# Attention, SiLU layer and rational layer on one core: forty instead of 23 products of zeros, and a new order of the work

## The chip, the core and the metric

One core of a Trainium2 chip. The time is device microseconds of one execution. The engines are PE (TensorE: products, and loads of its stationary operand), DVE (VectorE), ACT (ScalarE), POOL (GpSimd) and SP, which issues the DMAs. Each engine works through its own queue in order; semaphores tie the queues together.

## The reference

Input are 4 batches x 8 heads x 768 tokens with x (32 wide), a, B and C (16 wide). Three stages follow one another:

```
# attention, sub-chunks of 32 tokens, per batch and head
L = exp(cum_i - cum_j) for i >= j;  M = (C B^T) * L
y = M x + (C state) * exp(cum)
state = exp(sum la) * state + sum_j B_j x_j * exp(cum_end - cum_j)
# the heads side by side: 3072 tokens x 256
x1 = silu(y @ w_in) @ w_out                        # 256 -> 2048 -> 256
h  = x1 @ w_in2
x2 = (a0 + a1 h + a2 h^2 + a3 h^3) / (1 + |b0||h| + |b1| h^2 + 1e-6) @ w_out2
```

The kernel gets the layers' weights as 64-bit floats, and the rest as 32-bit floats.

## The kernel before

**Tiling.** The 3072 tokens are 24 chunks of 128. Attention goes chunk by chunk: C B^T and the masks (tile M, L700, two per chunk), the state (S and um, L780 to L792), y; y leaves as a high part y1h (ACT, L802) and a low part y1l (DVE, L805). Layer 1 runs over seven blocks of 2, 2, 4, 4, 4, 4, 4 chunks, and in each over sixteen slices f of 128 hidden units: 256 inputs to 128 hidden units (tile h), SiLU on ACT (L888), its high part gh (L844 on ACT or L846 on POOL) and low part gl (L850 on DVE or POOL), and the product back to 256 outputs, summed in acc over the slices. The first two blocks are 256 tokens wide, so their products are 128x256, the others 128x512. Layer 2 does the same over six blocks of 512 tokens with the rational function.

**Three products for one.** Each fp32 operand of the layers is split into a high and a low half that TensorE takes at full precision, and a product is hi·hi + lo·hi + hi·lo (in_proj L813, out_proj L819). All products are issued by mm, so they all show as L280.

**Weights.** A slice of weights arrives as 64-bit words (wraw, L472, 512 KB), becomes fp32 (wv) by one ACT instruction (L489) and two of DVE (L495, L497, below: the decode pair), and is split into the high half (ACT, L513) and the low half (L517, on POOL or DVE). A product with slice f needs both. The names w0 to w15 are the sixteen slices of layer 1. Factors Ee of later chunks are stored to memory (dre, L443) and loaded back spread out (L579); SP issues these and all other DMAs in one queue.

**The order.** No engine's order is written out by hand. Each step is handed to a planner (class Plan) with a list of engines that may do it, a cost on each, what it depends on, and a key. The planner runs a clock of its own: of all steps that could start soonest it takes the one with the smallest key, and this fixes the order of every engine before the program is built. The keys are sums of due times and of the numbers in the dictionary K (L31 to L69).

**Products of zeros.** K["warm"] steps are products of a 128x128 by a 128x512 tile of zeros in bf16, into a bank that is not in use (L452 to L460). POOL clears the zeros once (T, L450). Their key is 99.0, and each may begin from a time of its own on the planner's clock:

```
    for i in range(int(K["warm"])):
        ...
            mm(acc_t[1], z[:, 0:P], z[:, 0:512], True, True)
        add({"PE": (0.215, f_warm)}, 99.0, [o_zero], use=[zeros, spare], cols=512, after=K["warm0"] + K["warmstep"] * i)
```

In the trace they show as acc<-T, in the order as acc1<-T.

Of the kernel before, what the change touches and what calls it, by code (L numbers as in the profile page):

```python
# [28 lines left out]
HALVED = 0  # L29
TAIL_FLEX = 1  # L30
K = dict(  # L31
    t0=-18.163,
    step0=2.86,
    lag1=43.503,
    fo1=10.942,
    fo2=4472.323,
    fol=32.531,
    tab=-80.822,
    lead=168.696,
    kt=-12.237,  # L40
    kq=-77.043,
    kl=20.552,
    kg=62.898,
    ks=777.795,
    warm=23,
    warm0=5.147,
    warmstep=0.414,
    late=46.508,
    tab0=-2757.678,
    bulk=-58.119,  # L50
    d0=-14.734,
    gap0=36.588,
    d2=-19.542,
    d3=2.257,
    early2=9.278,
    early=24.026,
    w2a=-1512.003,
    w2b=-160.848,
    w1=-1.707,
    w1step=-31.741,  # L60
    w1load=3869.872,
    tokload=-233.083,
    ahead=17.68,
    eps=0.031,
    step2=168.582,
    dT=[-64.27, 36.68, -1.66, 34.6, -29.6, -174.18, 35.5, -3.13, -9.78, 138.44, -41.72, -26.53],
    dD=[-124.33, -53.44, 1.94, -60.08, -128.23, 35.27, -89.78, -84.57],
    dW=[28.05, -44.69, -91.49, 180.41, 166.11, 92.54, 19.47, 34.68, 21.96, 122.42, 25.71, 20.72, -50.06, -0.22, -24.39, 76.24],
)  # L69
SET_LN_EXP, SET_SILU = 6, 18  # L70

# [1098 lines left out]
```

## Time and profile before

| | |
|---|---|
| runs, us | 610.43, 612.09, 612.76; median 612.09 |
| profiled execution, us | 611.65, its span 609.9 |
| mean granted clock of TensorE | 0.985 |
| PE busy | 597.7 us, 98% of the span |
| DVE, ACT, POOL busy | 441.9, 401.2, 375.8 us |

The profile is of one execution. The span runs from its first to its last instruction; the time of the execution is 1.75 us more. A stretch's granted clock of 1.00 is TensorE's upper level, 2.4 GHz, 0.50 its lower, 1.2 GHz. In a row of a timeline neighbouring instructions of one kind stand together (x4), with the time from the first's start to the last's end, and in brackets the idle time before them and what ended it.

### The profile page before, as it was taken

The numbers are of one execution on the slowest core, as the hardware profiler recorded it, in microseconds if no ns is written. First come the engines' busy times: TensorE is split into PE (matmuls) and PEld (weight loads), VectorE is DVE, ScalarE is ACT, GpSimd is POOL, SyncE is SP. The second block draws the span as 40 slices with busy tenths as digits, with TensorE's granted clock in tenths as the row PEclk, the third lists the DMA queues.
The fourth block names the chain that finished last, engine by engine and source line by source line (L and its number), as shares of the span: only waits on it lengthen the run. The fifth ranks groups of instructions, "written<-read, shape, count | busy, mean of one in ns | idle before, by whom it ended". The sixth has DMA issues, their size and how long they took to land.

```text
span 609.9 us, 9980 instructions
## 1 busy us (share of the span) xinstructions
PE 597.7 (98%) x3501; PEld 478.6 (78%) x3505; DVE 441.9 (72%) x740; ACT 401.2 (66%) x782; POOL 375.8 (62%) x493
## 2 busy tenths in 40 slices
PE   7799999999999999999999999999999999999997
PEld 4478798887777777777888888888888788878875
DVE  5799988665344435432313899999999999999994
ACT  5678777554333333322335898989988988898893
POOL 5878846205344444222201599899889889889984
PEclk8599999999999999999999999999999999999999
DMA  7765778751111000000036600000000000000000
GB/s 258 227 199 209 234 250 286 243 200 37 46 28 36 23 21 27 1 2 1 1 104 199 250 0 1 36 1 1 35 1 2 34 1 1 35 1 1 35 2 34
DMA packets 18314, 47.30 MB, mean 78 GB/s; under 512 B 2136, under 2 KB 5336, under 8 KB 18264
## 3 DMA queue, kind: packets, MB, share of 16 engines
q1 hardware_dynamic: 18264, 46.67, 23.1%
q8 instruction: 27, 0.44, 0.3%
q14 instruction: 23, 0.19, 0.1%
HBM read 34.99 MB, written 11.67 MB: 77 GB/s over the span
## 4 chain that ended last, share of the span: by engine, by line
PE 88%; DVE 4%; DMA 4%; ACT 2%; issue 1%; SPq 0%; DVEq 0%; ACTq 0%
PE acc L280 42%; PE h L280 35%; PE b L280 7%; PE att L280 4%; DMA wraw<-in_w_dram 3%; DMA Ee<-dre 1%; DVE wv L497 1%; DVE w L517 1%; ACT wv L489 1%; DVE M L700 1%; DVE wv L495 0%; DVE gl L850 0%; ACT w L513 0%; DVE tok L613 0%; DVE y1l L805 0%
## 5 line engine op out<-in xcount | busy, mean ns | idle before, releaser
L280 PE MATMUL h<-y1h,w 128*128 128x512 f32 (+1 forms) x700 | 229.4, 377 | 2.3 <-DVE gl L850 1.9
L280 PE MATMUL acc<-gh,w 128*128 128x512 f32 (+1 forms) x832 | 213.1, 377 | 0.2 <-ACT gh L844 0.2
L280 PEld LDWEIGHTS acc<-gh,w 128*128 128x128 f32 x832 | 149.4, 188 | 30.6 <-POOL gh L846 0.4
L280 PEld LDWEIGHTS h<-y1h,w 128*128 128x128 f32 x700 | 129.7, 189 | 31.9 <-DVE gl L850 3.0
L850 DVE TENSOR_TENSOR gl<-T,gh 128x512 fp32r<-128x512 f32 x79 | 57.4, 727 | 116.0 <-POOL gh L846 84.8
L280 PE MATMUL h<-y1l,w 128*128 128x512 f32 (+1 forms) x350 | 130.8, 374 | 0.0
L850 POOL TENSOR_TENSOR gl<-g,gh 128x512 fp32r<-128x512 f32 x95 | 123.1, 1300 | 11.5 <-ACT gh L844 4.5
L280 PE MATMUL acc<-gl,w 128*128 128x512 f32 (+1 forms) x416 | 123.8, 378 | 0.0
L846 POOL TENSOR_SCALAR gh<-T 128x512 fp32r<-128x512 f32 x54 | 33.9, 627 | 137.2 <-ACT T L888 106.7
L888 ACT ACTIVATE T<-h 128x512 f32<-128x512 f32 x80 | 47.7, 597 | 97.6 <-PE h L280 91.8
L280 PEld LDWEIGHTS acc<-gl,w 128*128 128x128 f32 x416 | 75.9, 188 | 16.1
L953 POOL TENSOR_SCALAR tok<-T,abt 128x512 f32<-128x512 f32 x96 | 74.7, 778 | 16.3 <-ACT T L945 13.1
L280 PEld LDWEIGHTS h<-y1l,w 128*128 128x128 f32 x350 | 66.4, 190 | 11.6 <-DVE y1l L805 0.2
L956 DVE SCALAR_TENSOR_TENSOR b<-T,absb,b 128x512 f32<-128x512 f32 x96 | 71.9, 749 | 2.9 <-ACT b L949 2.6
L965 ACT ACTIVATE b<-b,lnb 128x512 f32<-128x512 f32 x96 | 64.1, 667 | 14.6 <-DVE b L956 14.6
L974 DVE SCALAR_TENSOR_TENSOR g<-tok,abt,b 128x512 f32<-128x512 f32 x96 | 71.3, 742 | 2.3 <-POOL gl L850 1.3
L590 POOL TENSOR_SCALAR_AFFINE_SELECT Gm<-eG 128x256 f32<-128x256 f32 x96 | 52.4, 581 | 9.8 <-ACT eG L386 6.0
L968 ACT ACTIVATE b<-b 128x512 f32<-128x512 f32 x96 | 56.8, 592 | 0.3
L962 DVE SCALAR_TENSOR_TENSOR tok<-T,abt,h 128x512 f32<-128x512 f32 x63 | 46.8, 743 | 0.9
L280 PE MATMUL b<-y1h,w 128*128 128x512 f32 x132 | 46.4, 392 | 0.0
L959 DVE TENSOR_TENSOR h<-tok,h 128x512 f32<-128x512 f32 x63 | 43.2, 686 | 0.0
L949 ACT ACTIVATE b<-h,abt 128x512 f32<-128x512 f32 x63 | 42.0, 667 | 0.9 <-DVE g L974 0.5
(76 smaller groups left out, 687.6 us busy)
## 6 DMA issues: line engine op xcount, KB each, us to landing
wraw<-in_w_dram SPq DMA_DIRECT2D x32, 512.0 KB, 5.1
w2s<-wraw SPq DMA_DIRECT2D x16, 512.0 KB, 3.4
w<-w2s SPq DMA_DIRECT2D x16, 512.0 KB, 4.2
tok<-in_tok_dram SPq DMA_DIRECT2D x24, 320.0 KB, 3.2
out_dram<-Gm SPq DMA_DIRECT2D x12, 256.0 KB, 2.0
Ee<-dre SPq DMA_DIRECT2D x21, 66.5 KB
cum<-in_consts_dram SPq DMA_DIRECT2D x1, 320.0 KB, 3.1
dre<-Ee SPq DMA_DIRECT2D x2, 66.5 KB
```

The costliest lines, as they stand in the source:

```text
L280: PE.matmul(out, lhsT, rhs, start=start, stop=stop)
L590: POOL.affine_select(g4[:, :, p * SUB : (p + 1) * SUB], eG[:, p, n * H : (n + 1) * H].unsqueeze(2).broadcast_to([P, H, SUB]), pattern=[[0, ...
L850: eng.tensor_tensor(gl.t[:, 0:W], g.t[:, 0:W], gh.t[:, 0:W], op=ALU.subtract)
L888: ACT.activation(T.t[:, 0:W], h.t[:, 0:W], AF.Silu)
L949: ACT.activation(c.t[:, 0:W], h.t[:, 0:W], AF.Abs, scale=abt[:, 4:5])
L953: POOL.tensor_scalar(t1.t[:, 0:W], s.t[:, 0:W], abt[:, 3:4], abt[:, 1:2], op0=ALU.mult, op1=ALU.add)
L956: DVE.scalar_tensor_tensor(c.t[:, 0:W], s.t[:, 0:W], absb[:, 1:2], c.t[:, 0:W], op0=ALU.mult, op1=ALU.add)
L959: DVE.tensor_tensor(h.t[:, 0:W], t1.t[:, 0:W], h.t[:, 0:W], op=ALU.mult)
L962: DVE.scalar_tensor_tensor(t1.t[:, 0:W], s.t[:, 0:W], abt[:, 2:3], h.t[:, 0:W], op0=ALU.mult, op1=ALU.add)
L965: ACT.activation(c.t[:, 0:W], c.t[:, 0:W], AF.Ln, bias=lnb)
L968: ACT.activation(c.t[:, 0:W], c.t[:, 0:W], AF.Exp, scale=-1.0)
L974: DVE.scalar_tensor_tensor(g.t[:, 0:W], t1.t[:, 0:W], abt[:, 0:1], c.t[:, 0:W], op0=ALU.add, op1=ALU.mult)
```

## The change

The dictionary K is replaced; no other line differs. warm goes from 23 to 40, the other numbers are keys (all but warm0 and warmstep differ):

```
-    t0=-18.163,
-    step0=2.86,
+    t0=-6.161,
+    step0=4.251,
...
-    warm=23,
+    warm=40,
     warm0=5.147,
     warmstep=0.414,
...
-    dD=[-124.33, -53.44, 1.94, -60.08, -128.23, 35.27, -89.78, -84.57],
+    dD=[-156.62, -40.06, -8.38, -62.34, -108.32, 38.34, -55.21, -111.62],
```

Every engine gets a new order. Apart from those of zeros the products on PE are the same as before, and the same ones stand ahead of slice 13 of block 0 and of slice 4 of block 1. In the names below the first number tells the tile and is the same in both programs where the tile is; the last number is a running one.

On PE, between slice 12 of block 0 (h_268) and its slice 13 (h_271), before:

```order
L280 MATMUL h_268_881<-y1h_67,w12_58_852 128x256 x2
L280 MATMUL h_268_881<-y1l_68,w12_58_852 128x256
L280 MATMUL h_268_881<-y1h_67,w12_58_852 128x256
L280 MATMUL h_271_895<-y1h_67,w13_61_865 128x256
L280 MATMUL h_271_895<-y1l_68,w13_61_865 128x256
L280 MATMUL h_271_895<-y1h_67,w13_61_865 128x256 x2
L280 MATMUL h_271_895<-y1l_68,w13_61_865 128x256
L280 MATMUL h_271_895<-y1h_67,w13_61_865 128x256
L280 LDWEIGHTS T_15_91
L280 MATMUL acc1_73<-T_15_91 128x512
```

Slice 13's products follow slice 12's at once, and five products of zeros (T_15) stand behind them, of which the first is shown. The same place after the change, from the last two of eleven products of zeros on:

```order
L280 LDWEIGHTS T_15_91
L280 MATMUL acc1_73<-T_15_91 128x512
L280 LDWEIGHTS T_15_91
L280 MATMUL acc1_73<-T_15_91 128x512
L280 MATMUL h_271_940<-y1h_67,w13_61_912 128x256
L280 MATMUL h_271_940<-y1l_68,w13_61_912 128x256
L280 MATMUL h_271_940<-y1h_67,w13_61_912 128x256 x2
L280 MATMUL h_271_940<-y1l_68,w13_61_912 128x256
L280 MATMUL h_271_940<-y1h_67,w13_61_912 128x256
L280 LDWEIGHTS T_15_91
```

Eleven products of zeros now stand between the two slices, and one follows; six more stand directly ahead of slice 12. In all 34 instead of 18 stand ahead of slice 13, and 40 instead of 23 ahead of slice 4 of block 1.

On DVE, what stands just ahead of the low half (L517) of slice 13 before:

```order
L497 SCALAR_TENSOR_TENSOR wv_57_755<-wraw_56_684,wv_57_755 128x512
L495 TENSOR_SCALAR wv_60_810<-wv_60_810 128x512
L850 TENSOR_TENSOR gl_267_854<-h_265_787,gh_266_820 128x256
L497 SCALAR_TENSOR_TENSOR wv_60_810<-wraw_59_751,wv_60_810 128x512
L517 TENSOR_TENSOR w12_58_852<-wv_57_755,w12_58_852 128x512
L517 TENSOR_TENSOR w13_61_865<-wv_60_810,w13_61_865 128x512
L805 TENSOR_TENSOR y1l_68<-att0_80,y1h_67 128x2x128
L788 TENSOR_TENSOR um_117_890<-att1_81,con_60 128x64
L700 TENSOR_TENSOR M_115_893<-att0_80,Gm_113_713 128x512
```

and after:

```order
L495 TENSOR_SCALAR wv_60_837<-wv_60_837 128x512
L805 TENSOR_TENSOR y1l_68<-att0_80,y1h_67 128x2x128
L700 TENSOR_TENSOR M_115_867<-att0_80,Gm_113_743 128x512
L700 TENSOR_TENSOR M_116_878<-att1_81,Gm_113_743 128x512
L850 TENSOR_TENSOR gl_267_884<-h_265_842,gh_266_872 128x256
L497 SCALAR_TENSOR_TENSOR wv_60_837<-wraw_59_778,wv_60_837 128x512
L495 TENSOR_SCALAR wv_63_894<-wv_63_894 128x512
L792 SCALAR_TENSOR_TENSOR S_114_915<-S_108_794,Ee_106_451,um_117_851 128x64
L497 SCALAR_TENSOR_TENSOR wv_63_894<-wraw_62_839,wv_63_894 128x512
L517 TENSOR_TENSOR w13_61_912<-wv_60_837,w13_61_912 128x512
L517 TENSOR_TENSOR w14_64_929<-wv_63_894,w14_64_929 128x512
```

The low half of slice 12 has left DVE for POOL, and two masks of chunk 8 (M_115, M_116), a state update (S_114) and slice 14's decode pair (wv_63) have moved ahead of slice 13's low half. Counted from the start, 107 instructions instead of 93 stand ahead of it.

On POOL, the early low halves of slices 1 and 2 before:

```order
L607 TENSOR_TENSOR tok_73_161<-tok_73_161,eL_66 128x128
L517 TENSOR_TENSOR w1_25_211<-wv_24_183,w1_25_211 128x512
L590 AFFINE_SELECT Gm_74_238<-eG_65 128x8x32 x4
L629 TENSOR_TENSOR tok_73_161<-tok_73_161,Ee_12_202 128x128
L517 TENSOR_TENSOR w2_28_258<-wv_27_226,w2_28_258 128x512
```

and on DVE after:

```order
L495 TENSOR_SCALAR wv_27_226<-wv_27_226 128x512
L517 TENSOR_TENSOR w1_25_217<-wv_24_183,w1_25_217 128x512
L497 SCALAR_TENSOR_TENSOR wv_27_226<-wraw_26_185,wv_27_226 128x512
L788 TENSOR_TENSOR um_78_245<-att1_81,con_60 128x64
L700 TENSOR_TENSOR M_71_250<-att0_80,Gm_69_178 128x512
L517 TENSOR_TENSOR w2_28_248<-wv_27_226,w2_28_248 128x512
```

The low halves of slices 1, 2, 3, 5, 7 and 9 move from POOL to DVE, and those of 11 and 12 the other way. In the rest of the kernel 41 high parts gh move from POOL to ACT, and the attention of chunks 12 to 15 moves to an earlier place. On SP the load of chunk 4's tokens now stands ahead of the first store of dre instead of behind it.

## Rows read from the trace of the kernel before

**Rows 1.** Page: busy time; tenths of 40 slices, ACT and clock.
```profile
PE 597.7 (98%) x3501; PEld 478.6 (78%) x3505; DVE 441.9 (72%) x740; ACT 401.2 (66%) x782; POOL 375.8 (62%) x493
...
ACT  5678777554333333322335898989988988898893
...
PEclk8599999999999999999999999999999999999999
```
**Rows 2.** Stretches: us, busy of PE, PEld, DVE, ACT, POOL; clock; DMA; GB/s.
```profile
15.00:28.50 13.50, 11.48 (x93) 6.92 (x90) 10.96 (x22) 8.44 (x19) 11.88 (x20) 0.50 0.76 229
30.00:45.00 15.00, 14.70 (x166) 11.47 (x167) 13.99 (x30) 10.81 (x27) 11.16 (x15) 1.00 0.66 203
45.00:60.00 15.00, 14.56 (x180) 12.36 (x178) 14.44 (x31) 12.54 (x36) 12.63 (x22) 1.00 0.65 216
60.00:75.00 15.00, 13.83 (x164) 11.58 (x161) 13.93 (x31) 11.80 (x32) 11.98 (x17) 1.00 0.66 218
75.00:90.00 15.00, 15.00 (x164) 14.27 (x157) 13.15 (x30) 12.73 (x35) 6.11 (x11) 1.00 0.75 244
```
**Rows 3.** Timeline of PE: start, us, instruction, idle before and what ended it.
```profile
24.98 0.58 PE L280 MATMUL h<-y1h,w 128*128 128x256 f32 x1
...
30.23 0.39 PE L280 MATMUL h<-y1h,w 128*128 128x256 f32 x1 [1.25 <-DVE gl L850]
...
34.59 1.03 PE L280 MATMUL acc<-T 128*128 128x512 bf16 x4
35.59 0.71 PE L280 MATMUL att<-tok 32*128 32x256 f32 x8
...
58.58 0.40 PE L280 MATMUL h<-y1h,w 128*128 128x256 f32 x2
...
59.65 1.03 PE L280 MATMUL acc<-T 128*128 128x512 bf16 x4
...
75.12 0.39 PE L280 MATMUL h<-y1h,w 128*128 128x256 f32 x1
```
**Rows 4.** Timeline of DVE, same columns.
```profile
29.55 0.29 DVE L613 TENSOR_TENSOR tok<-tok,Ee 128x128 f32<-128x128 f32 x1 [1.33 <-DMA Ee<-dre]
...
55.82 0.67 DVE L497 SCALAR_TENSOR_TENSOR wv<-wraw,wv 128x512 uint32<-128x512 uint32 x1
56.42 1.74 DVE L517 TENSOR_TENSOR w<-wv,w 128x512 fp32r<-128x512 f32 x2
```
**Rows 5.** DVE by lines, 15 to 75 us: count, busy us, mean ns, idle before.
```profile
L497 DVE SCALAR_TENSOR_TENSOR wv<-wraw,wv 128x512 uint32<-128x512 uint32 x17 | 12.9, 758 | 0.1
L700 DVE TENSOR_TENSOR M<-att,Gm 128x512 f32<-128x512 f32 x18 | 12.0, 676 | 0.0
L495 DVE TENSOR_SCALAR wv<-wv 128x512 uint32<-128x512 uint32 x17 | 9.1, 535 | 1.2 <-ACT wv L489 1.0
...
L517 DVE TENSOR_TENSOR w<-wv,w 128x512 fp32r<-128x512 f32 x6 | 4.9, 822 | 0.2
L613 DVE TENSOR_TENSOR tok<-tok,Ee 128x128 f32<-128x128 f32 x9 | 4.1, 454 | 1.5 <-DMA Ee<-dre 1.3
L805 DVE TENSOR_TENSOR y1l<-att,y1h 128x256 fp32r<-128x256 f32 x9 | 3.7, 415 | 1.9 <-ACT y1h L802 1.9
L792 DVE SCALAR_TENSOR_TENSOR S<-S,Ee,um 128x64 f32<-128x64 f32 x6 | 2.6, 431 | 0.0
L788 DVE TENSOR_TENSOR um<-att,con 128x64 f32<-128x64 f32 x5 | 1.1, 213 | 0.0
```
**Rows 6.** DVE by lines and shapes, whole span, same columns.
```profile
L651 DVE TENSOR_TENSOR cf<-tok,cf 128x128 fp32r<-128x128 f32 x1 | 0.3, 290 | 0.0
```
**Rows 7.** All of L517 on layer 1's slices: ns min/median/max, first and last start.
```profile
L517 POOL TENSOR_TENSOR w<-wv,w x9: 1268/1282/1298, 14.0 to 47.7; 128x512 fp32r<-128x512 f32 x9
L517 DVE TENSOR_TENSOR w<-wv,w x7: 693/889/910, 10.6 to 64.3; 128x512 fp32r<-128x512 f32 x7
```
**Rows 8.** Timeline of ACT, same columns.
```profile
21.29 0.67 ACT L489 ACTIVATE wv<-wraw 128x512 f32<-128x512 f32 x1 [2.45 <-DMA wraw<-in_w_dram]
```

More of the change, by code (lines that the diff above doesn't have):

```diff
@@ L31 @@
 K = dict(
-    t0=-18.163,
-    step0=2.86,
[L34 to L44, printed above, removed]
-    warm=23,
+    t0=-6.161,
+    step0=4.251,
+    lag1=39.738,
+    fo1=16.788,
+    fo2=24783.915,
+    fol=219.033,
+    tab=271.642,
+    lead=148.094,
+    kt=2.908,
+    kq=-189.812,
+    kl=56.621,
+    kg=110.576,
+    ks=-912.331,
+    warm=40,
     warm0=5.147,
     warmstep=0.414,
[L48 to L66, printed above, removed]
-    dD=[-124.33, -53.44, 1.94, -60.08, -128.23, 35.27, -89.78, -84.57],
-    dW=[28.05, -44.69, -91.49, 180.41, 166.11, 92.54, 19.47, 34.68, 21.96, 122.42, 25.71, 20.72, -50.06, -0.22, -24.39, 76.24],
+    late=71.039,
+    tab0=-11769.134,
+    bulk=16.473,
+    d0=-2.104,
+    gap0=11.268,
+    d2=-12.301,
+    d3=-0.756,
+    early2=20.723,
+    early=77.126,
+    w2a=-1396.273,
+    w2b=-420.014,
+    w1=4.464,
+    w1step=-47.488,
+    w1load=12566.424,
+    tokload=1745.097,
+    ahead=27.204,
+    eps=0.017,
+    step2=326.288,
+    dT=[-103.61, 16.78, -5.76, 49.19, -41.77, -160.95, 18.57, 63.77, -7.06, 213.65, -18.22, -7.06],
+    dD=[-156.62, -40.06, -8.38, -62.34, -108.32, 38.34, -55.21, -111.62],
+    dW=[6.31, -19.44, -118.33, 166.26, 142.84, 83.61, 9.81, 74.54, 6.21, 139.47, 10.23, -10.07, -65.84, 9.06, -101.93, 29.86],
 )
```

## Prediction

> **What bounds the kernel now.** I read the page's totals first [rows 1]: TensorE (PE) is busy 597.7 us of a span of 609.9, so at most 12.2 us are idle. Next come the stretches [rows 2]. From 75 us on PE is busy 15.00 of 15 us: there an engine beside it can cost time only by making PE wait, and an extra product costs its whole length. Before 75 us there are two losses. From 15 to 28.5 us the granted clock is 0.50, the lower of TensorE's two levels (1.2 of 2.4 GHz), and PE is idle 13.50 - 11.48 = 2.0 us as well. From 30 to 75 us the clock is full and PE is idle 0.30 + 0.44 + 1.17 = 1.9 us; a further 1.25 us is the wait ahead of 30.23 us for the first gl [rows 3]. VectorE (DVE) is what PE waits for there: it is busy 13.99, 14.44 and 13.93 of 15 us [rows 2], decoding weights and making masks. Ahead of 28.5 us it is not full: 10.96 of 13.50.
>
> The five zero products at 34.59 and the five at 59.65 us [rows 3] (one of each five is missing from the records) show where the order of before expects PE to wait. A zero product takes about 0.2 us: from 34.59 to the next product at 35.59 are five, 1.0/5 = 0.20; the four recorded ones span 1.03 us with a tail of one product, at most 1.03/4 = 0.26. I take 0.215.
>
> **The change part by part.** *Zero products.* Seventeen more, 17 x 0.215 = 3.66 us of PE time (3.4 to 4.4 by those bounds). The order shows where: 14 instead of 13 stand ahead of block 0's first product of slice 0, so the stretch at half clock gets one more; the five at 34.59 are gone; six stand ahead of slice 12, eleven directly ahead of slice 13, and six instead of five between there and slice 4 of block 1, 40 in all. The products that count are the same ones, and as many, ahead of each of these places.
>
> *DVE's queue.* I compare what stands ahead of slice 13's low half (L517 w13), which frees slice 13's products. It ends at 56.42 + 1.74 = 58.16 us [rows 4], and those products begin at 58.70, as the second in the row at 58.58 [rows 3]. After the change 17 instructions more and 3 fewer stand ahead: six low halves (w1, w2, w3, w5, w7, w9, from POOL) at 0.822, two cf low parts at 0.290, two L613 at 0.454, a y1l at 0.415, um at 0.213, two masks at 0.676, a decode pair 0.535 + 0.758, a state update 0.431; minus two low halves (w11, w12, to POOL) and one L613 [rows 5, 6]. That is 10.12 - 2.10 = 8.02 us. Neighbours on DVE overlap by 0.07 us (55.82 + 0.67 against 56.42 [rows 4]), so 14 instructions net give 8.02 - 0.98 = 7.04.
>
> How much lies in slack? Four low halves less one decode, 4 x 0.822 - 0.758 - 0.21 = 2.3 us, stand ahead of chunk 3's second mask, where DVE has 13.50 - 10.96 = 2.5 us idle and then 1.33 us for a DMA at 29.55 [rows 2, 4]. I cost them at nothing; without that cover they cost 2.3. The other 4.7 us fall where DVE is nearly full: idle are 1.0 us from 30 to 45 and 0.56 from 45 to 60 [rows 2]. With 1.5 regained, the low half ends 3.2 us later, at 61.4 (59.6, if the early waits are regained as well, to 65.2, if none is).
>
> *Both together at PE.* Without any waiting of its own PE reaches slice 13 with 34 - 18 = 16 more zeros, 16 x 0.215 = 3.4 us later, at 62.1; small gaps in 30 to 58 take back some tenths. The zeros thus just cover the longer wait for DVE (61.4), and PE arrives at about 62. From there to slice 4 of block 1 (75.12 us [rows 3]) DVE has four instructions fewer: a cf part more (0.290), and gone from there um, slice 14's decode pair, a state update and a layer-2 low half (0.213 + 0.535 + 0.758 + 0.431 + 0.693, the last at the shortest of rows 7), in all -2.34 + 0.28 = -2.1 us. PE can't use all of that: its products and zeros are fixed, and only the 1.17 us idle of 60 to 75 [rows 2] can go, while one more zero adds 0.2. By DVE alone slice 4 would start at 75.12 + 3.2 - 2.1 = 76.2; by PE at 75.12 + 3.66 less the idle that vanishes: 1.17, the 0.30 and 0.44 before, perhaps nothing of the wait for gl, so 1.9 in all. PE is the later: 75.12 + 3.66 - 1.9 = 76.9, **+1.8 us**. Bounds: +0.5 if the wait for gl and more goes too (3.66 - 1.9 - 1.25), +3.7 if no idle goes.
>
> *Ahead of 28.5 us.* What holds block 0's first product (24.98 [rows 3]) is on ScalarE (ACT): a weight decode waits 2.45 us for slice 4's words at 21.29 [rows 8], and behind it stand the table load, two high halves and chunk 1's y1h. All five still stand in that order. The queue of SP issues chunk 4's tokens ahead of the first store of dre now instead of behind it, so that slice 4's words have one transfer fewer between; but the store waits for an Ee that ACT makes two instructions later. I cost it at nothing (between -2.0, the whole idle time of the stretch, and +1).
>
> *Moves with one answer, nothing.* 41 high parts gh go from POOL to ACT in the blocks after the first two, where ACT is busy two to five tenths [rows 1]; attention of chunks 12 to 15 is computed some 50 us earlier, into a stretch where PE is full either way; from about 300 us the orders of PE agree. Cover: PE's full queue. If DVE, busy 13.15 of 15 from 75 to 90 [rows 2], falls late there, it costs up to its missing slack, of the order of 1 us.
>
> *A rule weighed.* A low half takes DVE 889 ns in the median and 693 at least, POOL 1282 [rows 7]: if that spread is what POOL's work beside it costs, it is 0.2 us each. The Trainium skill (SBUF — State Buffer, Who interferes with whom) says that the port pair of DVE and GpSimd is an exclusive lock and the loser blocks entirely. By that, taking six subtractions off POOL would give DVE up to 6 x 1.28 = 7.7 us back for the 4.9 it takes on, a gain of 2.8; by the row, 6 x 0.2 = 1.2, which doesn't pay. The row bears out a short hold, not a whole instruction's.
>
> **Sum.** The profiled execution took 611.65 us, 1.75 more than its span, and 0.44 less than the median of the runs (612.09). 611.65 + 1.8 = 613.4.
>
> **The rivals.**
> - *The waits only change places* (no change). All idle from 28.5 to 75 us, 1.9 + 1.25, becomes zeros, +0.5, or DVE gains a little from a quieter POOL: 611.7 to 612.4. For it: nearly all extra zeros stand where PE would wait anyway. Against: the first gl hangs on ACT and DVE, not on zeros.
> - *The early stretch gets shorter* (faster). w1 to w3 no longer wait for POOL, y1h and y1l of chunk 0 come earlier; if the 2.0 us idle there go too, on top of the case above (+0.5), and the clock rises 3 to 6 us earlier (PE then does in half the time what it did): 0.5 - 2.0 - 1.5 to 3.0 = -3.0 to -4.5 → 608.7 to 607.2. Against: the load and the table that hold the first product are where they were. A sentence beside it: the Trainium skill (TensorE: Matmul & The Clock Gate, Terms) puts the penalty at the throttled time times (1 - K/N); for the 13.5 us at half clock that would be an estimate of 6.75 us to win at most; the row's 2.0 us of idle say that part of the stretch would be waiting at the full clock.
> - *DVE doesn't regain its idle* (slower). If the low half of slice 13 ends at 65.2, PE has run out of zeros at 62.1 and waits 3 us; of the 1.17 us idle behind, less one zero, 0.95 comes back: 58.70 + 7.04 = 65.7 at the product, 7.0 - 0.95 = +6.1 → 617.7. It decides from slice 13 at 63.2 us on (63.2 - 58.7 - 0.95 = 3.5, the bound of slower below). For it: the added instructions stand behind the same loads; against: DVE's early idle of 3.8 us is real slack.
>
> **How the numbers follow.** My forecast 0.43 (612.7 to 614.9); waits change places 0.22; early stretch shorter 0.18; DVE late 0.17. About 0.5% (3.06 us) is what a measurement can tell from no change: faster is under 609.0, slower over 615.15. The early case ends below 609.0 in most of its weight (0.15), the rest of it is no change; the late case gives 0.14 of slower, the top of my forecast 0.03. So faster 0.15, same 0.68, slower 0.17. The range leaves out the far part of either side, about a tenth each: 608.4 to 616.4.
>
> **What would show it.** Right: slice 13's first product at about 62, zeros on PE right ahead of it with little idle time, slice 4 of block 1 near 76.9, the clock of 15 to 28.5 us again 0.50, 11 low halves of layer 1 on DVE. Wrong: block 0's first product well before 25 us, or a clock that rises earlier (faster); an idle stretch on PE behind the zeros with L517 on DVE as its releaser (slower); new idle time after 75 us, which I have put at nothing.

## The result and the profile after

The changed kernel takes 615.03 us (median of 6 runs, 613.77 to 616.21) against 611.21 us for the kernel before on the same chip (6 runs, 610.04 to 612.76): ratio 1.0063 [1.0049, 1.0077], 3.8 us slower. The forecast was 613.4, 1.8 us more on the profiled execution; the direction and the range held, the size was half of what came. The profiled execution of after took 616.21 us with a span of 614.5, 4.6 us more than the profiled one of before, and is the slowest of its six runs; so the traces have to explain 4.6 us, the medians 3.8.

The page of after, totals and two of the rows of tenths, against [rows 1]:

```profile
PE 600.2 (98%) x3522; PEld 481.2 (78%) x3522; DVE 440.5 (72%) x746; ACT 425.6 (69%) x819; POOL 356.8 (58%) x449
...
ACT  4667776875544444444433799998889899998983
...
PEclk9899999999999999999999999999999999999999
```

PE's idle time grew from 12.2 to 14.3 us (614.5 - 600.2), beside 2.5 us more of busy time. The stretches of after, columns as in [rows 2] (the second overlaps the third):

```profile
15.00:28.50 13.50, 7.80 (x86) 4.49 (x82) 10.58 (x25) 7.89 (x16) 7.61 (x13) 0.94 0.52 164
28.50:33.50 5.00, 5.00 (x43) 3.38 (x42) 4.49 (x10) 4.61 (x13) 3.69 (x6) 0.50 0.49 179
30.00:45.00 15.00, 13.56 (x153) 10.31 (x153) 12.02 (x28) 10.48 (x26) 9.38 (x16) 0.88 0.59 184
45.00:60.00 15.00, 14.73 (x182) 11.93 (x181) 15.00 (x32) 11.75 (x32) 13.95 (x22) 1.00 0.68 216
60.00:75.00 15.00, 14.87 (x137) 11.36 (x134) 14.45 (x29) 11.83 (x32) 10.29 (x15) 1.00 0.58 189
75.00:90.00 15.00, 14.69 (x193) 13.23 (x192) 12.25 (x29) 11.15 (x31) 8.30 (x14) 1.00 0.82 267
```

From 45 to 75 us PE is almost full, as forecast (idle 0.27 and 0.13 us, where it was 0.44 and 1.17). From 30 to 45 us it is idle 1.44 us instead of 0.30, and DVE is busy 12.02 us there instead of 13.99: the engine with the fuller queue does less. From 28.5 to 33.5 us PE is full at the lower clock, 0.50, where before the clock is 1.00 from 28.5 us on. PE's timeline of after (start, us, instruction, idle before and what ended it), at the places of [rows 3]:

```profile
26.02 0.32 PE L280 MATMUL att<-tok 128*32 128x64 f32 x8 [3.69 <-DVE um L788]
...
26.32 0.47 PE L280 MATMUL h<-y1h,w 128*128 128x256 f32 x1
...
42.55 0.45 PE L280 MATMUL att<-tok,S 32*64 32x128 f32 x8 [1.44 <-DVE y1l L805]
...
59.66 1.47 PE L280 MATMUL acc<-T 128*128 128x512 bf16 x6
...
62.39 2.55 PE L280 MATMUL acc<-T 128*128 128x512 bf16 x11
64.59 0.47 PE L280 MATMUL h<-y1h,w 128*128 128x256 f32 x1
...
80.02 0.39 PE L280 MATMUL h<-y1h,w 128*128 128x256 f32 x1 [0.31 <-DVE gl L850]
```

Block 0's first product starts at 26.32 (24.98 before), slice 13's at 64.59, right behind its eleven zeros (58.70), slice 4 of block 1 at 80.02 (75.12). All of the 4.6 us are there by then: +1.34, then up to slice 13 4.55 more, then -0.99, and -0.3 to the end of the span. The 1.44 us at 42.55 are followed back in the chain of waits of after, of 36 to 44 us (start, us, what):

```profile
34.04 5.68 DMA wraw<-in_w_dram
...
39.74 0.68 ACT wv L489
40.42 0.27 ACT y1h L802
...
40.72 0.04 DVE y1l L805
...
41.06 0.68 DVE M L700
41.74 0.34 DVE wv L495
42.08 0.34 DVE y1l L805
...
42.55 1.45 PE att L280 x28
```

Slice 8's words land at 39.72. ACT stands on their decode, chunk 3's y1h behind it; DVE is idle 1.86 us for that y1h, and the y1l that PE waits for stands behind on DVE, after a mask and a decode step. Those words held ACT for 1.71 us. The same wait for slice 4's words, at 21.29 in [rows 8], is in ACT's timeline of after:

```profile
23.26 0.66 ACT L489 ACTIVATE wv<-wraw 128x512 f32<-128x512 f32 x1 [1.45 <-DMA wraw<-in_w_dram]
```

The queue of SP, which issues the transfers in order, after:

```profile
18.41 0.33 SPq L443 DMA_DIRECT2D dre<-Ee  x1
18.85 0.37 SPq L472 DMA_DIRECT2D wraw<-in_w_dram  x1
...
26.19 0.60 SPq L579 DMA_DIRECT2D Ee<-dre  x1
32.90 0.33 SPq L561 DMA_DIRECT2D tok<-in_tok_dram  x1
...
34.04 0.90 SPq L472 DMA_DIRECT2D wraw<-in_w_dram  x2
```

and the same of before:

```profile
15.55 0.33 SPq L443 DMA_DIRECT2D dre<-Ee  x1
...
28.28 0.33 SPq L472 DMA_DIRECT2D wraw<-in_w_dram  x1
32.97 0.33 SPq L561 DMA_DIRECT2D tok<-in_tok_dram  x1
```

Before, slice 8's words are issued at 28.28, ahead of chunk 6's tokens, which can't go before 32.97 because their buffer is in use. After, they stand behind these tokens and go at 34.04 (the first of the two). The first store of dre goes at 18.41 instead of 15.55, since its Ee now stands behind slice 2's high half on ACT, and slice 4's words follow that store. DVE's idle time from 15 to 45 us grew from 4.6 to 6.0 us (30 less the third busy figure), first before, then after:

```profile
15.00:45.00 30.00, 26.66 (x263) 18.45 (x257) 25.40 (x53) 19.98 (x47) 23.82 (x36) 0.77 0.71 212
```

```profile
15.00:45.00 30.00, 22.86 (x244) 16.07 (x240) 23.97 (x55) 19.66 (x45) 17.42 (x30) 0.89 0.59 185
```

### The profile page after: what moved, and what is told of

Read it like the earlier page. It is cut to its first block, busy times and chain, and to the rows that moved or that the text cites. A ratio compares the mean times of both kernels' runs of the same rounds, so it can differ in the third digit from the quotient of the medians.

```text
span 614.5 us, 10135 instructions
## 1 busy us (share of the span) xinstructions
PE 600.2 (98%) x3522; PEld 481.2 (78%) x3522; DVE 440.5 (72%) x746; ACT 425.6 (69%) x819; POOL 356.8 (58%) x449
## 4 chain that ended last, share of the span: by engine, by line
PE 87%; DMA 5%; DVE 3%; issue 2%; ACT 1%; POOL 1%; SPq 0%; POOLq 0%; DVEq 0%; ACTq 0%
PE acc L280 42%; PE h L280 33%; PE b L280 7%; PE att L280 4%; DMA wraw<-in_w_dram 3%; DMA w2s<-wraw 1%; DVE wv L497 1%; DMA Ee<-dre 1%; DMA dre<-Ee 1%; DVE w L517 1%; ACT wv L489 0%; DVE wv L495 0%; POOL Gm L590 0%; DVE M L700 0%; ACT wraw L513 0%
## 5 line engine op out<-in xcount | busy, mean ns | idle before, releaser
L850 DVE TENSOR_TENSOR gl<-T,gh 128x512 fp32r<-128x512 f32 x73 | 52.5, 719 | 110.7 <-ACT gh L844 105.5
L846 POOL TENSOR_SCALAR gh<-T 128x512 fp32r<-128x512 f32 x13 | 8.5, 658 | 144.0 <-PE acc L280 141.8
L590 POOL TENSOR_SCALAR_AFFINE_SELECT Gm<-eG 128x256 f32<-128x256 f32 x96 | 57.2, 629 | 15.3 <-DVE M L700 7.7
L844 ACT ACTIVATE gh<-T 128x512 fp32r<-128x512 f32 x67 | 42.2, 630 | 27.7 <-PE acc L280 27.7
```

Of the source, the lines that this page charges most:

```text
L590: POOL.affine_select(g4[:, :, p * SUB : (p + 1) * SUB], eG[:, p, n * H : (n + 1) * H].unsqueeze(2).broadcast_to([P, H, SUB]), pattern=[[0, ...
L844: ACT.activation(gh.t[:, 0:W], g.t[:, 0:W], AF.Copy)
L850: eng.tensor_tensor(gl.t[:, 0:W], g.t[:, 0:W], gh.t[:, 0:W], op=ALU.subtract)
```

## The experiments

Two theories. *Zeros*: the seventeen are what costs, as in the forecast's sum, since the idle time that was to pay for them did not go. *Queues*: DVE, ACT and SP are late, and the zeros lie in PE's wait. In the expectations Z is the first; D (DVE's load), Q (SP's queue) and E (ACT's order) are parts of the second; P says that several of these hold PE at the same place, L that what is won early is lost again behind 75 us, A that all of the loss arises ahead of 75 us. All kernels but the last change the list of steps that the planner returns (their order, their engines or the zeros in it), just before the instructions are issued; `tag(op)` names a step, `at_(t)` is the place of step t in the list, `ahead` and `behind` move one step past another (`behind` with what hangs on it). This edit is common to all of them and is not repeated:

```
-    for op in plan.run():
-        fn = op.choices[op.eng][1]
-        fn()
+    order = plan.run()
...
+    for op in order:
+        op.choices[op.eng][1]()
```

Starts, in us, of the first product of block 0, of chunk 5, of slice 13 of block 0 and of slice 4 of block 1 in each trace; PE's products other than zeros ahead of these places are the same in all. Ratios are to the kernel before, run beside it:

| kernel | block 0 | chunk 5 | slice 13 | block 1, slice 4 | span | ratio |
|---|---|---|---|---|---|---|
| before | 24.98 | 41.19 | 58.70 | 75.12 | 609.9 | |
| after | 26.32 | 43.50 | 64.59 | 80.02 | 614.5 | 1.0063 [1.0049, 1.0077] |
| after, without 17 zeros | 26.05 | 42.69 | 62.51 | 80.72 | 615.2 | 1.0075 [1.0055, 1.0096] |
| after, low halves on POOL | 26.27 | 42.02 | 63.01 | 78.08 | 613.8 | 1.0077 [1.0064, 1.0089] |
| after, both | 25.60 | 42.27 | 61.59 | 79.85 | 615.1 | 1.0067 [1.0050, 1.0084] |
| before, with 17 zeros | 25.41 | 40.48 | 61.12 | 77.54 | 613.6 | 1.0054 [1.0042, 1.0066] |
| before, six low halves on DVE | 25.42 | 41.05 | 59.11 | 75.89 | 610.8 | 1.0021 [1.0007, 1.0034] |
| before, slice 8's words late | 24.54 | 42.65 | 60.73 | 77.17 | 612.7 | 1.0062 [1.0040, 1.0085] |
| after, slice 8's words first | 25.50 | 41.13 | 62.20 | 77.02 | 612.7 | 1.0051 [1.0034, 1.0067] |
| after, and the first Ee first | 24.37 | 40.95 | 62.03 | 77.50 | 613.5 | 1.0060 [1.0044, 1.0075] |
| that, DVE's order undone, with zeros | 25.07 | 41.52 | 62.61 | 77.97 | 613.1 | 1.0062 [1.0041, 1.0083] |
| that, without 17 zeros | 25.95 | 40.98 | 60.06 | 78.67 | 613.5 | 1.0059 [1.0043, 1.0075] |
| before, slice 4's words first | 24.88 | 40.03 | 57.07 | 73.59 | 608.7 | 0.9999 [0.9986, 1.0012] |
| before to 75 us, then new | 24.18 | 39.25 | 56.85 | 73.62 | 610.5 | 1.0009 [0.9997, 1.0022] |

**After without the 17 zeros** ahead of slices 12 and 13.

```
+    zeros_at = [i for i, op in enumerate(order) if tag(op) == ("zero",)]
+    skip = {order[i] for i in zeros_at[17:34]}
+    order = [op for op in order if op not in skip]
```

> The changed kernel, its order kept, without the 6 and the 11 products of zeros ahead of slices 12 and 13 of block 0. Theory Z (the zeros lie on PE's path): 17 x 0.215 = 3.7 us come back, 611.4 us. Theory D (DVE is late with slice 13's low half, at 64.6 us instead of 58.2, and the zeros only fill the wait): PE idles about 2.5 to 3.7 us ahead of slices 12 and 13 instead, the time stays at 614.5 to 615. Theory E (two ACT instructions in another order ahead of 45 us make everything late): as D here.

Nothing came back: 615.95. PE's timeline of this kernel shows waits where the zeros stood:

```profile
60.57 0.51 PE L280 MATMUL h<-y1h,w 128*128 128x256 f32 x2 [0.85 <-POOL w L517]
...
62.51 0.39 PE L280 MATMUL h<-y1h,w 128*128 128x256 f32 x1 [0.48 <-ACT w L513]
...
64.45 0.50 PE L280 MATMUL h<-y1h,w 128*128 128x256 f32 x2 [1.44 <-DVE w L517]
```

and its stretch has a lower clock, 0.89 (0.51 from 66.3 to 69.8 us, where four acc products take 1.05 us instead of 0.64):

```profile
60.00:75.00 15.00, 12.25 (x108) 10.39 (x109) 12.96 (x26) 10.40 (x28) 8.80 (x14) 0.89 0.41 146
```

In the changed kernel these zeros cover a wait, and with them the clock stays at 1.00 there. From block 0's first product to slice 4 of block 1 PE is idle 4.77 us without them and 2.68 with them, at clocks of 0.91 and 0.94. "Zeros" falls as an account of that kernel by itself.

**After with six low halves back on POOL**, and **both edits**.

```
+    for f in (1, 2, 3, 5, 7, 9):
+        order[at_(("lo", 0, f))].eng = "POOL"
```

> The changed kernel with the low halves of slices 1, 2, 3, 5, 7 and 9 put back on POOL, at the same place in the order, zeros as they are. Theory D alone: six subtractions of 0.82 us leave DVE, slice 13's low half ends 3 to 5 us earlier (60 to 62), and 611.5 to 612.5 us, unless the zeros hold PE until 64.7 in any case; then the time stays at 614.5 to 615 and only the low half is earlier. Theory Z: stays at 615. Theory E: 614 to 615.

> The changed kernel with both edits: without those 17 products of zeros and with the six low halves on POOL. If DVE and the zeros each hold PE until about 64.6 us (D and Z together), neither edit alone gains and both gain 3 to 4 us: 611 to 612. If only one of them holds, this is as that edit alone. If E holds, at most 1 us is gained.

615.89 and 615.57: neither edit, nor the two together, gives anything back. With both, POOL is busy 14.79 of 15 us from 45 to 60, and PE still waits 1.46 us for a low half on DVE, at 63.55. That zeros and low halves each hide the other is thereby refuted: something else in the queues is late too.

**Before with the 17 zeros**, six ahead of slice 12 and eleven ahead of slice 13.

```
+    zero = next(op for op in order if tag(op) == ("zero",))
+    for f, n in ((12, 6), (13, 11)):
+        i = at_(("in", 0, f))
+        order[i:i] = [zero] * n
```

> The kernel before, its order kept, with 17 more products of zeros, 6 ahead of slice 12 and 11 ahead of slice 13 of block 0, so 40 in all. There DVE delivers slice 13's low half at 58.2 us, so nothing waits in that place. Theory Z: 3.7 us less the idle time behind it of up to 1.2 us: +2.5 to +3.7 us, 613.7 to 615. Theory D or E as the whole cause: the zeros cost under 1 us.

614.71, +3.2 us (2.6 to 4.0 by the interval). PE has no wait there, and the zeros stand at their full length:

```profile
56.90 1.47 PE L280 MATMUL acc<-T 128*128 128x512 bf16 x6
...
58.92 2.55 PE L280 MATMUL acc<-T 128*128 128x512 bf16 x11
```

So the same seventeen products cost 3.2 us in one order, and taking them out of the other gives nothing back.

**Before with the six low halves on DVE** (the second edit's line with "DVE").

> The kernel before with the low halves of slices 1, 2, 3, 5, 7 and 9 on DVE instead of POOL, at the same place in the order. Theory D: six times 0.82 less what DVE has idle ahead of 45 us, slice 13's low half 2.5 to 4.5 us later than 58.2, 613.5 to 615.5. Theory Q: DVE takes them in its early idle time, at most +1 us (612.3).

612.37, +0.9 us by the medians (0.4 to 2.1 by the interval). DVE takes them in its idle time. The stretch of 15 to 45 us of this kernel:

```profile
15.00:45.00 30.00, 25.81 (x267) 17.91 (x265) 28.08 (x60) 21.04 (x52) 18.40 (x31) 0.84 0.70 211
```

Two places of DVE's timeline with low halves that were on DVE before as well:

```profile
31.86 0.68 DVE L517 TENSOR_TENSOR w<-wv,w 128x512 fp32r<-128x512 f32 x1
...
56.81 1.74 DVE L517 TENSOR_TENSOR w<-wv,w 128x512 fp32r<-128x512 f32 x2
```

and the first of them before (the second, 1.74 us as well, is in [rows 4]):

```profile
32.38 0.91 DVE L517 TENSOR_TENSOR w<-wv,w 128x512 fp32r<-128x512 f32 x1
```

DVE is busy 28.08 of 30 us instead of 25.40. The six low halves take 0.67 to 0.82 us each there, 4.2 in all. Where nothing else is late it does regain its idle time, as the forecast had it.

**Before with slice 8's words late** on SP, as after, and **after with them first**.

```
+    behind(("words", 0, 8), ("Ee", 7))
```

> The kernel before with slice 8's words put behind chunk 6's tokens and chunk 7's Ee on SP, as the change has them. Theory Q: +1 to +2 us, 612.5 to 613.5. Theory D: within 0.5 us of before, since y1h's wait would be taken up in DVE's slack.

614.60, +3.2 us (2.4 to 5.2 by the interval) from one transfer's place; no other step changes its place. ACT and PE of this kernel:

```profile
38.20 0.68 ACT L489 ACTIVATE wv<-wraw 128x512 f32<-128x512 f32 x1 [4.02 <-DMA wraw<-in_w_dram]
```

```profile
41.64 0.45 PE L280 MATMUL att<-tok,S 32*64 32x128 f32 x8 [2.57 <-DVE M L700]
```

The chain of after, alone: transfer, decode on ACT, what stands behind it there, DVE, PE. Behind this wait the granted clock falls once more, to 0.52 from 42.5 to 46 us, so part of the 3.2 us is the lower clock.

```
+    ahead(("words", 0, 8), ("tokens", 6))
```

> The changed kernel with one transfer moved on SP: the words of slice 8 ahead of the tokens of chunk 6, which wait until 32.9 us for PE to free a buffer. In the changed kernel slice 8's words are issued at 34.0 us (before: 28.3), ACT stands on their decode at 39.74, and chunk 3's y1h behind it, which costs PE 1.44 us at 42.55. Theory Q (the queue's order ahead of 45 us makes the rest late): chunk 5's first product 1.4 to 1.9 us earlier than 43.50, slice 13's low half about as much earlier, 613.2 to 613.8 us against 615.0. Theory D (DVE's load alone): no more than 0.5 us, 614.5 to 615.

614.75: chunk 5 starts 2.4 us earlier than in after (41.13; 0.8 of this is there at block 0's first product, ahead of the moved transfer), slice 13 as well, and 1.8 us of that are left in the span; of the ratios, 1.0051 beside 1.0063, the intervals overlap.

**And the first Ee ahead of slice 2's high half on ACT.**

```
+    ahead(("words", 0, 8), ("tokens", 6))
+    ahead(("bulk", 0), ("hi", 0, 2))
```

> As the last one, and on ACT the factors Ee for chunks 3 and up (L422, the first of the two that are stored to memory) ahead of slice 2's high half, as before. The store then goes at about 17 us instead of 18.4, slice 4's words and block 0's first product come about 1.2 us earlier (25.1 instead of 26.32). Theory Q: 612.0 to 612.8 us. Theory D: 614 to 615, since slice 13's low half still ends after 63 us.

615.22. Block 0's first product starts at 24.37, earlier than before, and chunk 5 is where it was before, yet slice 13 stands at 62.03: 3.3 us late, which is the zeros. Both repairs of the front work and the kernel is no faster.

**DVE's order undone as well**, with the zeros and without the seventeen: chunk 8's two masks and its state update and the second decode step of slice 14 go behind slice 13's low half again, as before.

```
+    for t in (("mask", 8, 0), ("mask", 8, 1), ("S", 8), ("bits", 0, 14, 1)):
+        behind(t, ("lo", 0, 13))
```

> The same with the 17 products of zeros. Theory P: PE has nothing left to wait for and the zeros lie on its path, slice 13 at 61.5 to 62.2, 2 us more than the run without: 614 to 615.2. Theory L: as the run without, 614 to 615.

> The changed kernel with three moves undone (slice 8's words and the stored Ee first, as in the run before; on DVE the two masks of chunk 8 and the second decode step of slice 14 behind slice 13's low half instead of ahead of it) and without the 17 products of zeros ahead of slices 12 and 13. Theory P (several things hold PE at the same place, so that undoing one shows nothing: the queue's order, DVE's order and the zeros): slice 13's low half ends 2 us earlier than 62.0, slice 13 starts at 59.5 to 60.5, 612.0 to 613.2 us. Theory L (what is won ahead of 60 us is lost again behind 75, where the attention of chunks 12 to 15 now stands): 614 to 615.

614.79 and 615.06. Without the zeros slice 13 comes at 60.06, as expected, but not the gain behind it. PE and the stretch of this kernel:

```profile
63.61 0.35 PE L280 MATMUL h<-y1h,w 128*128 128x256 f32 x1 [1.85 <-DVE gl L850]
```

```profile
60.00:75.00 15.00, 12.87 (x124) 10.32 (x124) 13.28 (x27) 9.94 (x27) 9.06 (x14) 0.89 0.50 171
```

The time won at slice 13 becomes a wait for the next gl, and a lower clock.

**Before with slice 4's words ahead of the first store**, a try at a faster kernel: it takes away the wait of [rows 8].

```
+    ahead(("words", 0, 4), ("store", 0))
```

> The kernel before with one transfer moved on SP: slice 4's words ahead of the first store of Ee, which waits until 15.55 us while the DMA engines stand idle. If the queue decides the early stretch, slice 4's decode no longer waits 2.45 us at 21.29, block 0's first product comes 1 to 2.5 us before 24.98, and 609.0 to 610.5 us against 611.4. If what is won there becomes another wait ahead of 60 us: 611 to 612.

611.18 against 611.32: no change. The decode's wait at 21.29 is gone, and ACT waits later for DVE, on the same chain:

```profile
23.31 0.63 ACT L513 ACTIVATE w<-wv 128x512 fp32r<-128x512 f32 x1 [1.61 <-DVE wv L497]
```

**Before up to slice 4 of block 1, then the new order.** FIRST lists the steps and engines of before's order up to there, with its zeros of that part; the new planner orders the rest, without zeros.

```
+    names = {"P": "PE", "A": "ACT", "D": "DVE", "G": "POOL", "S": "SP"}
+    first = [(plan.ops[int(x[1:])], names[x[0]]) for x in FIRST.split()]
+    for op, eng in first:
+        op.eng = eng
+    done = {op for op, _ in first}
+    order = [op for op, _ in first] + [op for op in order if op not in done and getattr(op, "tag", None) != ("zero",)]
```

> A kernel put together from both orders: the old order of every engine, with its 23 products of zeros, up to slice 4 of block 1 (75 us), and the new order for all that is left, without further zeros. Theory A (all of the loss arises ahead of 75 us: SP's and DVE's order and the zeros, each of which hides the others): 611.0 to 611.9 us, as before. Theory L (the new order behind 75 us, with the attention of chunks 12 to 15 at 75 to 115 us, costs PE on its own what the single edits won): 612.5 to 614.

612.18, +0.5 us (-0.2 to +1.3): by the medians 3.3 of the change's 3.8 us arise ahead of 75 us, by the unfavourable ends of both intervals (3.0 and 1.3) at least 1.7. What is left shows as waits of PE for gl, first where the two orders meet, and again, 1.11 us, at 95.57:

```profile
77.89 0.39 PE L280 MATMUL h<-y1h,w 128*128 128x256 f32 x1 [1.15 <-DVE gl L850]
```

## Why the prediction came out as it did

**Zero products**: the term was about right. Seventeen at 0.215 were 3.66 us. From chunk 5 to slice 13 after needs 64.59 - 43.50 = 21.09 us and before 17.51, 3.58 more, and nineteen zeros stand there instead of none: 0.19 each, 3.2 for seventeen. On the kernel before seventeen cost 3.2 us as well.

**"Less the idle that vanishes: ... 1.9 in all"**: this is the step that failed. The 1.17 and 0.44 behind 45 us did go (to 0.13 and 0.27), and so did the 1.25 for the first gl, but other waits came: 1.44 us at 42.55 for chunk 3's y1l, and 0.53 for a y1l at 27.31, behind block 0's first product. From that product to slice 4 of block 1 PE is idle 2.94 us before and 2.68 after: 0.26 went instead of 1.9. At slice 4 of block 1 that makes +4.90 instead of +1.8: 1.34 ahead of block 0's first product, and behind it PE needs 53.70 us instead of 50.14, +3.56, close to the bound of +3.7 "if no idle goes", which I had taken for the range's end only.

**A cost that the sum lacks: the lower clock behind the first product.** The way from block 0's first product to chunk 5, columns as in [rows 2], first before, then after:

```profile
24.98:41.19 16.21, 14.89 (x153) 11.55 (x154) 14.69 (x31) 11.55 (x29) 12.26 (x18) 0.89 0.62 183
```

```profile
26.32:43.50 17.18, 15.21 (x154) 11.77 (x150) 14.07 (x32) 11.81 (x29) 9.84 (x16) 0.80 0.68 220
```

Clocks of 0.89 and 0.80 are about 3.6 and 6.9 us at the lower level. After needs 0.97 us more, though one zero stands there instead of five (0.8 us less); PE's idle time is 0.65 us more (1.32 and 1.97). What is left, 0.97 + 0.8 - 0.65 = 1.1 us, is an estimate of what the longer stretch at the lower clock costs. The parts of the +3.56 are then sixteen zeros at 0.19, 3.0 us, and 1.1 for the clock, less 0.26 of idle, 3.9 in all; what took the other 0.3 back isn't known. That +3.56 came so near the bound of +3.7 is in part luck: the bound has no term for the clock.

The same shows in "PE reaches slice 13 ... at 62.1": it does at 64.59, later by 2.5. The first product's 1.34, the clock's 1.1 and 0.55 us more of idle (0.65 up to chunk 5, then 0.10 less) are a little more than this.

**DVE's queue, "with 1.5 regained"**: wrong. The low half of slice 13 ends at about 64.7 (the first of a pair):

```profile
63.81 1.72 DVE L517 TENSOR_TENSOR w<-wv,w 128x512 fp32r<-128x512 f32 x2
```

where 61.4 was forecast, with 65.2 "if none is" regained. (The lower end, 59.6, would be 59.8 by its own idle times: 2.54 + 1.33 + 1.01 + 0.56 = 5.44 of 7.04 us.) The mechanism of the third rival held, and not its price: that one had PE waiting at slice 13 at 65.7 and the end at 617.7, but the zeros, and the wait at 42.55, fall into the same 3 us. I had counted DVE's instructions and not what feeds them. The run with six low halves on the kernel before shows that the slack was real (+0.9 us for 4.2 us of work), and the run with slice 8's words late shows one thing that uses it up: SP's order, +3.2 us by itself.

**Ahead of 28.5 us, "I cost it at nothing (between -2.0 ... and +1)"**: a further, smaller failure. I saw that the first store waits for an Ee made later, and stopped there; the store moved by 2.86 us, and slice 4's words behind it. Block 0's first product is 1.34 us later in this trace. A single trace is not good for that much: five traces with before's order up to there (before, and the rows with 17 zeros, six low halves, slice 8's words late, and new from 75 us) have it from 24.18 to 25.42, mean 24.9; five with after's (after, the next three rows, slice 8's words first; two of these and one of those have low halves on the other engine) from 25.50 to 26.32, mean 25.9. That makes 1.0 us.

**"The clock of 15 to 28.5 us again 0.50"**: wrong, it is 0.94. That was no forecast to make from one trace: before's own order up to 30 us has 0.75, 0.65, 0.63 and 0.87 there in four further traces. In after PE works only 7.80 of these 13.50 us, at the upper level for the most part, and the lower one comes with block 0's first products and stays longer than before: 0.50 from 28.5 to 33.5 us, with PE full. The eight traces with after's early order reach the full clock between 29 and 34 us, the six with before's between 27 and 30 us.

**The rule weighed** (the Trainium skill, SBUF — State Buffer, Who interferes with whom): the section calls the shared port pair an exclusive lock. It states the full block for the two-port modes; of an instruction with two inputs from SBUF, such as this subtraction, it says that it contends with GpSimd's reads. By a full block the move of six subtractions would have given DVE up to 2.8 us back; on the kernel before, DVE's busy time grew by 2.8 us (441.9 to 444.7), and the kernel took 0.9 us more. Of the seven low halves that stayed on DVE one got shorter, from 0.91 to 0.68 us, and the others kept their lengths, such as the pair of 1.74 us: the spread of 0.2 us from which the forecast read POOL's part is there without these subtractions too. No low half of layer 1 on DVE takes over 1.0 us in any trace here, where waiting for a whole instruction of POOL would add up to 1.28 to 0.68: the measurement decides against a whole instruction's wait here.

**Right**: eleven low halves on DVE, PE full from 45 to 75 us, slice 13's product directly behind its zeros, and 0.99 us given back behind it (0.95 forecast); the moves behind 75 us cost 1.3 us at most, by the interval. **The other rivals**: that the waits only change places asked for +0.5 us and is excluded by the interval; the early stretch got longer, not shorter.

**What stays open.** Single parts put on the kernel before cost 3.2 (zeros), 3.2 (slice 8's words) and 0.9 us (low halves); taking single parts out of the changed one gives nothing that its intervals show. So the parts hide one another: where one wait is taken out, the next is already late. The kernel with repaired front, undone DVE order and no zeros stays at 615. Its way from block 0's first product to slice 4 of block 1:

```profile
25.95:78.67 52.72, 48.89 (x530) 39.65 (x527) 47.23 (x102) 39.36 (x103) 39.03 (x60) 0.93 0.64 206
```

It starts 1.0 us later than before and needs 2.6 us more, which is all of its span's 3.6. Of the 2.6, 0.9 is idle time of PE (3.83 instead of 2.94), and about 4 us more are at the lower clock (0.93 instead of 0.96 over the way; 0.51 from 64.5 to 68 us, behind the wait of 1.85 us): an estimate of up to 2 us. Why PE waits there longer, with the six low halves on DVE and later decodes of slices 8 and 9, no run separates, and no run holds the clock up without zeros. No kernel here beats the one before.

## What to carry to other kernels

A filler product is free only while something else is late, and the price of a moved queue is free only while something covers it; cost each on the order where the others don't happen, and take the sum's upper bound seriously when several are moved at once. Before counting on idle time of an engine, follow its feeders through every queue, the DMA queue to its end, past each transfer that waits for a buffer: one transfer's place was worth 3.2 us. A wait of PE can cost more than its length, if the lower clock follows. And read the clock of a short stretch from several traces or not at all.

## What the runs showed of the hardware

- A transfer that waits for its buffer holds all behind it on SP's queue: 26.8 to 32.90 us in after, with slice 8's words behind it, which before stood ahead of that transfer and went at 28.28.
- Behind some waits of PE the granted clock falls: 0.89 instead of 1.00 from 60 to 75 us when the zeros go and 2.6 us of busy time with them (14.87 to 12.25), and 0.52 from 42.5 to 46 us behind the wait of 2.57 us when slice 8's words are late. Behind the 1.44 us at 42.55 in after it does not: 1.00 from 43.5 to 64.59 us.
- After's early order stays longer at the lower clock behind block 0's first product: 0.50 from 28.5 to 33.5 us, 1.00 there before.
- The clock's record misses the lower level at the start. Its first 15 us in after read 1.00, yet zeros take 3.17/7 = 0.45 us each at 1.20 us, against 2.55/11 = 0.23 at 62.39, and the ten products with cum 2.32 us, where before has 1.27. PE of after:

```profile
1.20 3.17 PE L280 MATMUL acc<-T 128*128 128x512 bf16 x7 [1.20 <-POOL T L450]
...
5.72 2.32 PE L280 MATMUL h<-la,cum 128*128 128x32 f32 x10 [0.91 <-DMA cum<-in_consts_dram]
```

its first stretch (the record of the clock is the 1.00):

```profile
0.00:15.00 15.00, 12.29 (x75) 8.26 (x75) 7.06 (x17) 7.09 (x18) 7.19 (x19) 1.00 0.78 268
```

and PE of before:

```profile
4.94 1.27 PE L280 MATMUL h<-la,cum 128*128 128x32 f32 x10 [0.16 <-DMA cum<-in_consts_dram]
```

Which of the two it is varies from trace to trace with after's early order (2.31 or 2.32 us in five of eight traces, 1.27 in two, 1.70 in one), and is 1.27 in all six with before's; so these ten products alone differ by 1.05 us between traces of one early order. Block 0's first product shows less of it: 26.05 without the 17 zeros (1.27) and 26.32 and 26.27 in after and with the low halves on POOL (2.32).
